# V of two batches loaded in four DMAs each, and casts on VectorE moved to earlier half-steps

## The chip, the cores and the metric

The kernel runs on one NeuronCore of a Trainium2 chip. The metric is the device time of the whole kernel in microseconds (us), median over several runs. The names of the engines are those of the profile: PE is the matrix engine, PEld its weight loads, DVE is VectorE, ACT is ScalarE, POOL is GpSimd, SP is SyncE, which here only issues DMAs.

## What is computed

Eight batches of attention with eight heads, 576 positions and head dimension 64, each query seeing itself and the 63 keys before it; the result, laid out as 4608 tokens of width 512, goes through two matrix products with an activation between them.

```python
scores = scale * q @ k.T ; scores = where((i - j >= 0) & (i - j < 64), scores, -1e9)
attn = softmax(scores) ; x = (attn @ v) as [4608, 512]
h = x @ w_in                       # [4608, 2048]
out = (h - tanh(h)) @ w_out        # [4608, 512]
```

Inputs and the output are float32. The kernel computes in bf16 with float32 sums.

## The kernel before

**Units of work.** A batch `b` has four pairs of heads; pair `pr` of batch `b` is unit `g = 4 b + pr`. The tokens are cut into nine chunks `c` of 512. For every chunk there are 16 steps `m` of the hidden layer: `hp_mm(c, m)` (four matrix products, L383), the tanh on ACT (L388), and `g_sub(c, m)`, the subtraction on DVE (L395) that writes `gT`. The second product (L407) reads `gT` and `w_out_sb`.

**The order.** The schedule is written out by hand. The program counts half-steps `h`. In `OPS`, step `m` of chunk 0 is at `h = 2 m`, step `m` of chunk 1 at `h = 32 + 2 m`. `at(h, fn, ...)` hangs other work on a half-step. In a half-step the matrix products and the tanh are recorded first, then what hangs there in the order of the `at` calls, and then the subtraction; each engine runs its instructions strictly in that order. Ahead of half-step 0 stands a prologue that does all of batch 0 (units 0 to 3).

**From DRAM to the matrix engine.** POOL issues the loads of q, k and v, which turn float32 into bf16 on the way: `load` one pair of q or k (L96), `load_v_all` the whole V of a batch (L135), `load_v` one pair of V (L143). All V of a batch goes to one tile, `vall`, of which there is one buffer. `cast_pair(g, eng)` copies k and q of unit `g` into rows that PE can transpose (`kb`, `qb`), `cast_v(b, pr, eng)` copies a pair of V into `vb`; both show at L85, on DVE or on POOL. When all four pairs of `vb` are there, `keys_v` sends it to `vw` in nine DMAs (L165), on POOL's and SP's queues in turn. `shift_dve(b, 0, 4)` copies `vw` by one block on DVE (L171), and `tile_pv` (L304) reads it. `tr_rows` transposes `kb` and `qb` on PE (L269), `tile_scores` is the score product and the exponential (L288, L291).

**Batch 1** (units 4 to 7): its V is loaded by the prologue, behind the first half of `w_in` (`wi`, one of two DMAs of L180) and ahead of units 4 and 5, the second half of `w_in`, and units 6 and 7. Its four `cast_v` hang on half-steps 1, 3, 5 and 9, `cast_pair` of unit 4 on 8, of unit 5 on 11, of units 6 and 7 on 16. `keys_v` of batch 1 is on 9, `shift_dve` on 18. The second half of `w_in` is first read by step `m = 8`, on half-step 16.

**Batch 2** (units 8 to 11): on half-step 9 POOL issues its V and then k and q of units 8 to 11. On half-step 21 POOL does its four `cast_v` and the casts of unit 8, which `tr_rows` of unit 8 needs on half-step 31. On half-step 23 come its `keys_v`, then `w_out` in two DMAs (L188) and q, k and V of batch 3 as three whole loads.

**The eight lanes of POOL's DMAs.** The built program gives each DMA of POOL's queue one of eight semaphores in turn (DMASW0 to DMASW7). A DMA therefore waits at POOL until the DMA eight places before it in POOL's queue has landed, and whatever stands behind it on POOL, DMAs and casts, waits too.

Of the kernel before, what the change touches and what calls it, by code (L numbers as in the profile page):

```python
# [15 lines left out]
def kernel(  # L16
# [11 lines left out]
    NP = H // 2  # L28
# [104 lines left out]
    def load_v_all(b):  # L133
        t = v_pool.tile([PV, H, EV * D], BF16, tag="v", name="vall")
        nc.gpsimd.dma_start(out=t, in_=v[b].rearrange("h (p e) d -> p h (e d)", e=EV))  # L135
        for pr in range(NP):
            stage[b, pr, "v"] = t[:, pr::NP]

    def load_v(b, pr):
        if (b, "v") not in whole:  # L140
            whole[b, "v"] = v_pool.tile([PV, H, EV * D], BF16, tag="v", name="vall")
        t = whole[b, "v"][:, pr::NP]
        nc.gpsimd.dma_start(out=t, in_=v[b, pr::NP].rearrange("h (p e) d -> p h (e d)", e=EV))  # L143
        stage[b, pr, "v"] = t
# [18 lines left out]
    def keys_v(b, j, eng=nc.sync):  # L163

        eng.dma_start(out=vw[b % 2][64:128, j].rearrange("p h c -> p (h c)"),  # L165
                      in_=vb[8 * j:8 * j + 8].rearrange("p e h c -> p e (h c)"))
# [12 lines left out]
    def load_w_in(i):  # L179
        nc.gpsimd.dma_start(out=w_in_sb[i], in_=w_in_r[:, :, 1024 * i:1024 * i + 1024])  # L180
# [260 lines left out]
    def at(h, fn, *args):  # L441
        items.setdefault(h, []).append((fn, args))
# [10 lines left out]
    V, A, G, Y = nc.vector, nc.scalar, nc.gpsimd, nc.sync  # L453
# [23 lines left out]
    for j, eng in enumerate((G, G, G, Y, G, Y, G, Y, G)):  # L477
        keys_v(0, j, eng)
    load_w_in(0)
    load_v_all(1)  # L480
    for g in 4, 5:
        load(g, "k", G)
        load(g, "q", G)
# [37 lines left out]

    at(0, lambda: nc.vector.memset(vw[1][0:64, 0], 0.0))
    at(0, lambda: nc.vector.memset(qT[1], 0.0))
    for pr, h in enumerate((1, 3, 5, 9)):
        at(h, cast_v, 1, pr, V)
    at(9, lambda: [keys_v(1, j, (G, Y)[j % 2]) for j in range(NJ)])
    at(8, cast_pair, 4, V)
    at(11, cast_pair, 5, V)
    at(9, load_v_all, 2)
    for g in 8, 9, 10, 11:  # L530
        at(9, load, g, "k", G)
        at(9, load, g, "q", G)
# [42 lines left out]
    for g in range(2 * NP + 2, B * NP):  # L575
        b, pr = divmod(g, NP)
# [96 lines left out]
```

## Time and profile before

| what | us |
|---|---|
| median of 7 runs | 335.42 (333.59 to 337.11) |
| the profiled execution | 335.42 |
| its span in the profile | 333.7 |
| PE busy in the span | 314.9 (94%) |
| DVE, ACT, POOL busy | 198.7, 184.1, 115.2 |

The span runs from the first to the last instruction; all places in time below are us from its start. The timeline gives for each instruction its start, its duration, the engine, the line, what it writes and reads, and in brackets the idle time of the engine before it with what ended it. A row that ends with "to landing" says how long a DMA took from the start of its issue to its arrival.

Where the loads of POOL's queue were issued and when they landed in this execution (us):

| DMA | issued | landed |
|---|---|---|
| `wi`, first half | 14.05 | 25.4 |
| V of batch 1 | 15.24 | 28.9 |
| k4, q4, k5, q5 | 16.44, 17.09, 17.72, 18.41 | 29.6, 30.4, 31.1, 31.9 |
| `wi`, second half | 19.23 | 36.8 |
| k6, q6, k7, q7 | 20.01, 25.74, 29.19, 29.93 | 37.6, 38.8, 40.2, 41.4 |
| five `vw` of batch 1 | 33.59 to 37.85 | 41.6 to 42.7 |
| V of batch 2 | 39.16 | 46.6 |
| k8 | 40.74 | 47.0 |
| q11 (the last of batch 2) | 46.88 | 53.1 |

### The profile page before, as it was taken

The numbers are of one execution on the slowest core, as the hardware profiler recorded it, in microseconds if no ns is written. First come the engines' busy times: TensorE is split into PE (matmuls) and PEld (weight loads), VectorE is DVE, ScalarE is ACT, GpSimd is POOL, SyncE is SP. The second block draws the span as 40 slices with busy tenths as digits, with TensorE's granted clock in tenths as the row PEclk, the third lists the DMA queues.
The fourth block names the chain that finished last, engine by engine and source line by source line (L and its number), as shares of the span: only waits on it lengthen the run. The fifth ranks groups of instructions, "written<-read, shape, count | busy, mean of one in ns | idle before, by whom it ended". The sixth has DMA issues, their size and how long they took to land.

```text
span 333.7 us, 6238 instructions
## 1 busy us (share of the span) xinstructions
PE 314.9 (94%) x2408; PEld 175.7 (53%) x2439; DVE 198.7 (60%) x335; ACT 184.1 (55%) x337; POOL 115.2 (35%) x167
## 2 busy tenths in 40 slices
PE   6867999899999999999999999999999999999996
PEld 2544565455555655655555555555554444444444
DVE  4576597993347675767676766677666433444400
ACT  3644779583466666666566666555553444434411
POOL 8842589604940843631724493500000000000000
PEclk9589999999999999999999999999999999999999
DMA  8999996995698289575975977966104000100022
GB/s 159 164 173 206 165 181 110 187 201 105 123 185 167 28 150 216 111 110 136 145 152 116 157 139 159 200 155 167 55 33 102 34 31 35 60 33 31 31 82 78
DMA packets 47222, 40.68 MB, mean 122 GB/s; under 512 B 18632, under 2 KB 40584, under 8 KB 47000
## 3 DMA queue, kind: packets, MB, share of 16 engines
q0 software_dynamic: 21440, 19.73, 39.1%
q1 hardware_dynamic: 25544, 20.25, 23.8%
q8 instruction: 19, 0.31, 0.4%
q10 hardware_dynamic: 208, 0.29, 0.3%
q14 instruction: 11, 0.09, 0.1%
HBM read 36.70 MB, written 10.62 MB: 142 GB/s over the span
## 4 chain that ended last, share of the span: by engine, by line
PE 73%; DVE 9%; DMA 8%; ACT 3%; POOL 3%; issue 2%; DVEq 0%; POOLq 0%
PE ps L407 34%; PE ps L383 28%; DMA vall<-in_v_dram 4%; PE ps L332 3%; PE ps L316 3%; DVE gT L395 2%; DMA vw<-vb 2%; DVE xs L343 2%; PE ps L249 2%; DMA qall<-in_q_dram 2%; DVE qt L85 2%; ACT qt L83 1%; PE ps L422 1%; DVE vw L171 1%; POOL vb L85 1%
## 5 line engine op out<-in xcount | busy, mean ns | idle before, releaser
L383 PE MATMUL ps<-xT,wi 128*128 128x512 bf16 x576 | 147.1, 379 | 2.7 <-DMA wi<-in_moe_w_in_dram 1.2
L395 DVE TENSOR_TENSOR gT<-ps,th 128x512 bf16<-128x512 f32 x144 | 98.5, 689 | 69.9 <-ACT th L388 68.6
L407 PE MATMUL ps<-w_out_sb,gT 128*128 128x512 bf16 x531 | 135.6, 379 | 1.5
L388 ACT ACTIVATE th<-ps 128x512 f32<-128x512 f32 x144 | 86.0, 599 | 82.3 <-PE ps L383 79.4
L383 PEld LDWEIGHTS <-wi 128*128 128x128 bf16 x576 | 60.4, 113 | 47.6 <-issue 3.2
L407 PEld LDWEIGHTS <-gT 128*128 128x128 bf16 x560 | 52.2, 98 | 52.7 <-issue 0.5
L318 ACT ACTIVATE pt<-ps 128x384 bf16<-128x384 f32 x66 | 32.3, 490 | 23.8 <-PE ps L316 23.8
L85 POOL COPY vb<-vall 72x1024 bf16<-72x1024 bf16 x24 | 24.8, 1054 | 35.0 <-DMA vall<-in_v_dram 35.0
L343 DVE TENSOR_TENSOR xs<-ps,rc 64x576 bf16<-64x576 f32 x44 | 33.2, 755 | 1.1
L412 ACT ACTIVATE ysb<-ps 128x512 f32<-128x512 f32 x35 | 21.0, 599 | 18.9 <-PE ps L407 18.8
L85 DVE COPY qt<-ps 64x576 bf16<-64x576 bf16 x18 | 13.7, 760 | 24.1 <-ACT qt L83 24.1
L85 POOL COPY qb<-qall 96x768 bf16<-96x768 bf16 x23 | 19.5, 846 | 19.5 <-DVE pt L322 10.5
L332 PEld LDWEIGHTS <-pt 128*128 128x128 bf16 x198 | 16.5, 98 | 15.3 <-DVE pt L322 0.8
L332 PE MATMUL ps<-vw,pt 128*128 128x130 bf16 x198 | 22.0, 220 | 0.4 <-DVE pt L322 0.4
L316 PE MATMUL ps<-qt,kt 128*128 128x128 bf16 x198 | 21.8, 219 | 0.0
L316 PEld LDWEIGHTS <-kt 128*128 128x128 bf16 x198 | 15.4, 98 | 8.8 <-issue 0.2
L85 POOL COPY kb<-kall 96x768 bf16<-96x768 bf16 x23 | 19.5, 850 | 1.2 <-DMA kall<-in_k_dram 1.2
L322 DVE TENSOR_TENSOR pt<-pt,ps 128x1152 bf16<-128x1152 bf16 x22 | 16.4, 745 | 0.8 <-ACT pt L318 0.8
L83 ACT ACTIVATE kt<-ps 128x576 bf16<-128x576 bf16 x22 | 14.4, 653 | 1.6 <-PE ps L249 1.5
L291 ACT ACTIVATE pt<-ps 128x640 bf16<-128x640 f32 (+1 forms) x20 | 12.5, 647 | 3.1 <-PE ps L288 3.1
L96 POOL DMA_DIRECT2D qall<-in_q_dram x15 | 9.9, 662 | 8.0 <-DMA wi<-in_moe_w_in_dram 5.1
L83 ACT ACTIVATE qt<-ps 64x576 bf16<-64x576 bf16 x18 | 11.5, 637 | 1.4 <-PE ps L249 1.4
(76 smaller groups left out, 202.7 us busy)
## 6 DMA issues: line engine op xcount, KB each, us to landing
out_dram<-ysb SPq DMA_DIRECT2D x35, 256.0 KB
vall<-in_v_dram POOLq DMA_DIRECT2D x7, 576.0 KB, 12.2
vw<-vb SPq DMA_DIRECT2D x39, 65.0 KB
qall<-in_q_dram POOLq DMA_DIRECT2D x4, 576.0 KB, 12.4
kall<-in_k_dram POOLq DMA_DIRECT2D x4, 576.0 KB, 12.5
kall<-in_k_dram POOLq DMA_DIRECT2D x15, 144.0 KB, 6.3
qall<-in_q_dram POOLq DMA_DIRECT2D x15, 144.0 KB, 5.8
wi<-in_moe_w_in_dram POOLq DMA_DIRECT2D x2, 1024.0 KB, 14.5
```

The source lines that it names most:

```text
L83: nc.scalar.activation(o, i, ACT.Copy)
L85: eng.tensor_copy(o, i)
L316: nc.tensor.matmul(sp[:, i, :], kT[g % NK][:, 64 * j:64 * j + 128], qT[g % NR][:, :, 64 * j:64 * j + 64], start=True, stop=True)
L318: nc.scalar.activation(PT[g % NPT][:, 3 * grp:3 * grp + 3, :], sp, ACT.Exp, scale=scale)
L322: nc.vector.tensor_tensor(p, p, mask.unsqueeze(1).to_broadcast([128, 2 * NJ, 64]), ALU.mult)
L332: nc.tensor.matmul(ps[:, 5 + grp, 130 * i:130 * i + 130], PT[g % NPT][:, j, :], vw[b % 2][:, j, 2 * pr:2 * pr + 2, :], start=True, stop=True)
L343: nc.vector.tensor_tensor(xo[r, :, :, pr, :], ov[r, :, :, h, 0:D], rc[r].to_broadcast([64, 3, 3, 64]), ALU.mult)
L383: nc.tensor.matmul(hp, w_in_tile(ki, m), chunk_tile(c)[:, :, ki % 2, 64 * (ki // 2):64 * (ki // 2) + 64], start=(ki == 0), stop=(ki == 3))
L388: nc.scalar.activation(th, hp, ACT.Tanh)
L395: nc.vector.tensor_tensor(gT[c][:, m, :], hp, th, ALU.subtract)
L407: nc.tensor.matmul(yp, gT[c][:, m, s * 128:(s + 1) * 128], w_out_sb[:, m, :], start=(m == 0), stop=(m == M - 1))
L412: nc.scalar.activation(ysb, ps[:, yp_bank(c, s), :], ACT.Copy)
```

## The change

V of batches 1 and 2 is loaded by four `load_v`, one for each pair, where one `load_v_all` stood. Two `cast_v` of batch 1 move to half-step 0, ahead of the first subtraction, the other two to half-steps 1 and 3. `cast_pair` of unit 4 moves from half-step 8 to 5, of unit 5 from 11 to 9.

```diff
     load_w_in(0)
-    load_v_all(1)
+    for pr in range(NP):
+        load_v(1, pr)
     for g in 4, 5:
         load(g, "k", G)
         load(g, "q", G)
...
-    for pr, h in enumerate((1, 3, 5, 9)):
+    for pr, h in enumerate((0, 0, 1, 3)):
         at(h, cast_v, 1, pr, V)
     at(9, lambda: [keys_v(1, j, (G, Y)[j % 2]) for j in range(NJ)])
-    at(8, cast_pair, 4, V)
-    at(11, cast_pair, 5, V)
-    at(9, load_v_all, 2)
+    at(5, cast_pair, 4, V)
+    at(9, cast_pair, 5, V)
+    for pr in range(NP):
+        at(9, load_v, 2, pr)
     for g in 8, 9, 10, 11:
         at(9, load, g, "k", G)
         at(9, load, g, "q", G)
```

The order on DVE from the end of the prologue, before and after (s0 is the first subtraction, V0 to V3 are the casts of V, kt the copies of transposed k out of PSUM):

```
before: s0 V0 s1 V1 s2 V2 s3 k4 q4 s4 V3 kt4 s5 k5 q5 s6 kt5 s7 k6 q6 k7 q7 s8
after:  V0 V1 s0 V2 s1 V3 s2 k4 q4 s3 s4 k5 q5 kt4 s5 s6 kt5 s7 k6 q6 k7 q7 s8
```

On POOL the one DMA of V becomes four in two places and nothing else moves; with it, the lane on which each later DMA waits moves by three. PE, ACT and SP keep their order.

## The prediction

> **What bounds the kernel now.** I read the busy shares, then PE's timeline over half-steps 0 to 31, then the landings of the DMAs that PE waits for, then POOL's timeline. First PE's row and its row of slices:
>
> ```profile
> PE 314.9 (94%) x2408; PEld 175.7 (53%) x2439; DVE 198.7 (60%) x335; ACT 184.1 (55%) x337; POOL 115.2 (35%) x167
> PE   6867999899999999999999999999999999999996
> ```
>
> PE is the bound; only its gaps can be won. Two rows of the windows (duration, then busy time by engine) show what the changed half-steps hold:
>
> ```profile
> 25.50:32.10 6.60, 5.53 (x24) 2.63 (x24) 4.01 (x10) 3.38 (x6) 1.91 (x3) 1.00 1.22 206
> 32.10:36.90 4.80, 4.27 (x55) 2.61 (x55) 4.31 (x10) 2.58 (x5) 2.17 (x3) 1.00 1.04 175
> ```
>
> PE idles 1.07 and 0.53 us there, DVE is busy 4.31 of 4.80. That speaks for the change. Now PE's timeline, the rows that count:
>
> ```profile
> 32.14 0.43 PE L269 MATMUL ps<-ident,kb 96*128 96x96 bf16 x6 [1.11 <-DVE kb L85]
> 36.55 0.43 PE L269 MATMUL ps<-ident,qb 96*128 96x96 bf16 x6
> 36.90 1.05 PE L383 MATMUL ps<-xT,wi 128*128 128x512 bf16 x4
> 42.50 1.02 PE L383 MATMUL ps<-xT,wi 128*128 128x512 bf16 x4 [0.24 <-DVE gT L395]
> 52.36 0.43 PE L269 MATMUL ps<-ident,kb 96*128 96x96 bf16 x6 [0.24 <-POOL kb L85]
> ```
>
> The gap at 32.14 is the wait for DVE's cast of k4. But 36.90 is step m = 8, the first that reads the second half of w_in, and that DMA has only just come:
>
> ```profile
> L180 POOL DMA_DIRECT2D wi<-in_moe_w_in_dram x1: 778/778/778, 19.2 to 19.2; - x1
> DMA to landing us min/median/max: 17.6/17.6/17.6
> ```
>
> 19.23 + 17.6 = 36.83, 0.07 before PE starts. So PE is on time for its data at 36.90; whatever it gains earlier, it waits for there. From 36.90 to 52.12 it idles 0.24 us once, at 42.50, for s8, which stands on DVE behind the cast of q7 (landed 41.4). At 52.36 it waits 0.24 for POOL's cast of k8. POOL up to there:
>
> ```profile
> 39.16 0.84 POOL L135 DMA_DIRECT2D vall<-in_v_dram  x1 [0.75 <-DMA qall<-in_q_dram]
> 40.74 0.67 POOL L96 DMA_DIRECT2D kall<-in_k_dram  x1 [0.74 <-PE ps L269]
> 41.95 0.65 POOL L96 DMA_DIRECT2D qall<-in_q_dram  x1 [0.54 <-PE ps L288]
> ...
> 45.18 0.63 POOL L96 DMA_DIRECT2D kall<-in_k_dram  x1
> 46.88 0.63 POOL L96 DMA_DIRECT2D qall<-in_q_dram  x1 [1.07 <-DMA vall<-in_v_dram]
> 47.51 4.03 POOL L85 COPY vb<-vall 72x1024 bf16<-72x1024 bf16 x4
> 51.48 0.82 POOL L85 COPY kb<-kall 96x768 bf16<-96x768 bf16 x1
> ```
>
> Ten issues, then four casts of V, then k8: an unbroken chain, and PE already waits at its end. The gaps at 40.74 and 41.95 are the lanes of k7 and q7 (landed 40.2 and 41.4), whatever releaser the row names; the one at 46.88 is V's own lane.
>
> **The change part by part.** *Casts on DVE.* V's casts last 0.42 us each on DVE, those of k and q 0.35 (0.34 and 0.27 from start to start). From the table of landings POOL's loads land in order of issue: V took the stream from 25.4 to 28.9, so I estimate pieces at 26.3, 27.2, 28.0 and 28.9. V0 and V1 are then done at 27.6, before s0, which started at 28.08 because its tanh was ready then. After it: V2, s1 (29.1), V3 (29.8 to 30.1), s2, k4 and q4 (30.75 to 31.3, landed at 29.6 and 30.4), s3, s4, k5 and q5 (32.6 to 33.1, landed 31.9). vb is complete at 30.1 in place of 33.3, k4 comes 1.0 us sooner, k5 about 1.9. PE's 1.6 us of gaps largely go, and PE stands at m = 8 near 35.4. There it waits for w_in until 36.83: gain 0.07 at most. The next tie is s8 behind q7's landing, gain 0; the next is k8 from POOL, the third part. So this edit I cost at nothing; what hides it is the second half of w_in. If that cover were gone, it would be worth up to 1.6 us. The other way: a piece of V that lands late holds s0 behind V1; up to some 1.4 us of that is covered by the same wait.
>
> *V of batch 1 in four.* A piece of V in the prologue cost POOL 0.68 to 0.83 us to issue (0.69 taken), the whole 0.85: 4 x 0.69 - 0.85 = 1.9 us more. Three more DMAs also shift the lanes: q5 now waits for the first half of w_in (lands 25.4) and is issued near 25.7, not 18.4; w_in's second half waits for V0 (26.3) and is issued near 26.6, not 19.2; k6, q6, k7, q7 near 27.5, 28.3, 29.2 and 29.95 (before: 20.0, 25.7, 29.2, 29.9). Cover: the stream was full until 41.4, and w_in's turn comes when q5 has landed, 31.9. Its issue ends at 27.4, 4.5 us ahead. So cost nothing; with the cover gone, each us of delay at w_in is one us at 36.90, of which the part that PE waits at 52.36 anyway is free. The vw DMAs on SP start some 3 us sooner, but must pass through the same stream before q7 either way; those on POOL stay behind q7 in the queue, and fourth and fifth wait for w_in and k6 as before (three more DMAs stand ahead of both, so the lanes fall alike).
>
> Here a rule speaks against the change. The Trainium skill, "SBUF — State Buffer", section "Who interferes with whom", says that a DVE copy in a two-port mode and GpSimd exclude each other for the whole instruction, and that descriptor generation counts as GpSimd's work. The trace has such a case:
>
> ```profile
> 58.95 1.22 POOL L135 DMA_DIRECT2D vall<-in_v_dram  x1
> 59.10 3.23 DVE L171 COPY vw<-vw 64x2080 bf16<-64x2080 bf16 x2
> ```
>
> The issue took 1.22 where others take 0.84, the two copies 3.23 where shift_dve of batch 0 took 1.52. By the rule the six casts that now fall between 26 and 31.5 can each hold an issue for one cast, 0.35 to 0.42: some 2 us on POOL in all, still within the 4.5 of cover. By the row, 0.4 for one collision. Both give 0 in the sum.
>
> *V of batch 2 in four.* This one has no cover. V0 goes at 39.16 as before (lane of q6), V1 on k7's lane at 40.5 to 40.7, V2 on q7's at 41.75 to 41.95, V3 at once, done 43.1 to 43.3. Then eight loads at 0.645: seven end at 47.6 to 47.8. The last, q11, waits for the lane of V3. Before, the two gaps at 40.74 and 41.95 were also there, but between them POOL issued k8 and q8; these now come after. When V3 lands isn't in the trace. Lower bound: the whole V landed at 46.6, then there is no wait. Upper: k10 flew 7.2 us, giving 49.7. Nearest rows: the pieces in the prologue flew 5.1 to 5.4, q8 to q9 5.6 to 5.8 in a full queue; I take 5.2 from 42.5, so 47.7, and 0.3 from landing to issue as at 46.56 to 46.88. Then q11 is issued at 48.0, the casts of V begin at 48.6, k8 at 52.6 and is ready near 53.4. Before: 47.51, 51.48, 52.3. POOL is 1.1 us later (0.75 without any wait for V3), and PE, in front of this wait before, is later by the same 1.1.
>
> Here too a rule is to hand: the Trainium skill, "DMA: Bandwidth & Descriptors", "Anatomy of one DMA — SWDGE (gpsimd) path", fits a DMA as about 2.0 us plus its bytes at 436 GB/s. Three more DMAs would be 6 us if one followed the other, against 3 x 0.65 of POOL's time by the rows. The landings in a full queue (k8 47.0, q8 47.6, k9 48.3) are 0.6 to 0.7 apart, so the fixed part overlaps; I count issue time only.
>
> Behind 52.36 everything hangs on the same POOL chain or on PE: qb8, five vw, w_out (landed 66.7 and 71.9, first read 75.20), the loads of batch 3. All shifts together, so nothing is given back. **Sum:** 0 + 0 + 1.1 = +1.1 us on the profiled execution of 335.42, which equals the median: 336.5.
>
> **The rivals.** *A, forecast:* the gain stops at w_in, POOL pays near k8: 336.5, own range 335.4 to 337.6; chance 0.55.
>
> *B, slower by more than the bound:* V3 of batch 2 lands late and the lane holds q11, and behind it the four casts and k8. With the 5.2 us as 7.2, as k10 flew, q11 goes at 50.0, POOL is 3.1 late: 338.5. It decides once V3 flies longer than about 5.8 us (casts begin after 49.2). For it: flights of 5.6 to 7.2 in that stretch. Against: V's pieces would have fewer loads ahead of them than k10 had. Chance 0.23.
>
> *C, a changed meeting of shift_dve and POOL at 59:* the copies start 1.1 us before POOL's casts at 60.17. A few tenths of drift frees them (gain about 1.5 of PE's waits at 62 to 65: 335.0) or catches both copies (loss about 1.9: 338.4). In the trace both sides hang on k8, so drift is small. Chance 0.12, split evenly.
>
> *D, faster:* the profile's own chain runs through V's landing at 28.9, vb and vw to 42.1. If that is the true path, and w_in and POOL do not hold it back, all of PE's gaps from 25.5 to 52.4 could go, 1.07 + 0.53 + 0.24 + 0.24 = 2.1: 333.3. Against: 36.83 beside 36.90, and the chain on POOL. Chance 0.10.
>
> **How the numbers follow.** A measurement of this kernel tells about 0.5%, 1.7 us, from no change: below 333.7 is faster, above 337.1 slower. Faster: D, and a little of C, 0.11. Slower: B 0.23, C's loss 0.06, and A's upper end 0.07: 0.36. Same: 0.53. The range takes A whole, B to just above its price, and most of C: 334.2 to 338.6, which leaves out D and a longer flight.
>
> **What would show it.** Right: PE at m = 8 still starts near 36.9, now after a wait of over 1 us for w_in; kb8 at PE near 53.4 with a wait of over 1 us on POOL; POOL's casts of batch 2 near 48.6; the loads still landing in order. Wrong: m = 8 near 35.5 (w_in was no gate), k8 cast before 51.5, or w_in landing after 38 (the late issue did starve the stream).

## Result and the profile after

The changed kernel took 336.28 us (median of 27 runs) against 335.78 for the kernel before (64 runs beside it): ratio 1.0019, 95% interval 1.0003 to 1.0035. That is 0.6 us more, within what I called no change; the forecast was 1.1 us more. A second set of 22 runs gave 0.9997 (0.9972 to 1.0022). The first profile of the changed kernel fell in a disturbed execution, so what is read below is the profile of that second set (called the rerun, span 334.5 us).

The page of the rerun, its busy shares and PE's slices:

```profile
PE 318.6 (95%) x2439; PEld 176.9 (53%) x2439; DVE 199.7 (60%) x335; ACT 184.3 (55%) x337; POOL 118.7 (35%) x173
PE   7877998799999999999999999999999999999996
```

POOL is busy 3.5 us more than before (118.7 against 115.2): six more DMA issues of 0.6 to 0.7, and little besides. PE's sum can't be compared with the 314.9 of before, because 31 matmul records are missing there (x2408 against x2439).

PE's timeline in the rerun, at the same places as before:

```profile
25.92 5.37 PE L383 MATMUL ps<-xT,wi 128*128 128x512 bf16 x24 [1.97 <-DMA wi<-in_moe_w_in_dram]
...
32.84 1.02 PE L383 MATMUL ps<-xT,wi 128*128 128x512 bf16 x4 [0.77 <-DVE gT L395]
...
36.93 1.05 PE L383 MATMUL ps<-xT,wi 128*128 128x512 bf16 x4 [0.46 <-DMA wi<-in_moe_w_in_dram]
...
52.99 0.43 PE L269 MATMUL ps<-ident,kb 96*128 96x96 bf16 x6 [1.08 <-POOL kb L85]
```

The wait of 1.11 us for DVE's cast of k4 is gone. In its place stands a wait of 0.77 for a subtraction (0.17 before), and then, at step m = 8, a new wait of 0.46 that names the DMA of w_in. That DMA:

```profile
L180 POOL DMA_DIRECT2D wi<-in_moe_w_in_dram x1: 764/764/764, 26.8 to 26.8; - x1
DMA to landing us min/median/max: 10.1/10.1/10.1
```

It was issued at 26.8, 7.6 us later than before, and landed at 36.9, as before: its later issue cost nothing. Between the waits at 36.93 and 52.99 PE ran without a pause. The wait for POOL's cast of k8 grew from 0.24 to 1.08. POOL's timeline ahead of it:

```profile
40.08 3.03 POOL L143 DMA_DIRECT2D vall<-in_v_dram  x4 [0.96 <-DMA qall<-in_q_dram]
43.10 0.67 POOL L96 DMA_DIRECT2D kall<-in_k_dram  x1
...
47.51 0.64 POOL L96 DMA_DIRECT2D qall<-in_q_dram  x1
48.14 4.04 POOL L85 COPY vb<-vall 72x1024 bf16<-72x1024 bf16 x4
52.11 0.82 POOL L85 COPY kb<-kall 96x768 bf16<-96x768 bf16 x1
```

Twelve issues without a gap (before: nine, with three gaps), then the casts: POOL's own issue time reaches from the landing of q6 to the casts. They begin at 48.14 (before: 47.51, forecast 48.6). But the first of these rows stands at 40.08, where it stood at 39.16 before, because q6 landed later. The account of the prediction below comes back to this.

### The profile page after: what moved, and what is told of

It is laid out like the page before. It is cut to its first block, busy times and chain, and to the rows that moved or that the text cites. A ratio compares the mean times of both kernels' runs of the same rounds, so it can differ in the third digit from the quotient of the medians.

```text
span 337.2 us, 6244 instructions
## 1 busy us (share of the span) xinstructions
PE 316.5 (94%) x2408; PEld 176.8 (52%) x2439; DVE 199.4 (59%) x335; ACT 184.2 (55%) x337; POOL 119.3 (35%) x173
## 4 chain that ended last, share of the span: by engine, by line
PE 72%; DMA 10%; DVE 8%; POOL 4%; ACT 3%; issue 2%; DVEq 0%; POOLq 0%
PE ps L407 31%; PE ps L383 30%; DMA vw<-vb 6%; DMA wi<-in_moe_w_in_dram 4%; PE ps L332 3%; DVE gT L395 2%; PE ps L316 2%; DVE xs L343 2%; PE ps L249 2%; DVE qt L85 1%; PE ps L422 1%; POOL vw L165 1%; DVE vw L171 1%; POOL vall L143 1%; PE ps L269 1%
## 5 line engine op out<-in xcount | busy, mean ns | idle before, releaser
L383 PE MATMUL ps<-xT,wi 128*128 128x512 bf16 x576 | 148.6, 383 | 5.5 <-DMA wi<-in_moe_w_in_dram 3.7
L332 PEld LDWEIGHTS <-pt 128*128 128x128 bf16 x198 | 16.5, 98 | 15.5 <-DVE pt L322 0.8
L332 PE MATMUL ps<-vw,pt 128*128 128x130 bf16 x198 | 22.2, 220 | 0.5 <-DVE pt L322 0.4
L165 POOL DMA_DIRECT2D vw<-vb x17 | 10.1, 601 | 6.0 <-DMA wi<-in_moe_w_in_dram 2.8
```

The costliest lines, as they stand in the source:

```text
L332: nc.tensor.matmul(ps[:, 5 + grp, 130 * i:130 * i + 130], PT[g % NPT][:, j, :], vw[b % 2][:, j, 2 * pr:2 * pr + 2, :], start=True, stop=True)
L383: nc.tensor.matmul(hp, w_in_tile(ki, m), chunk_tile(c)[:, :, ki % 2, 64 * (ki // 2):64 * (ki // 2) + 64], start=(ki == 0), stop=(ki == 3))
```

## The experiments

| run | what differs from the kernel before | ratio | 95% interval |
|---|---|---|---|
| again | the whole change | 0.9997 | 0.9972 to 1.0022 |
| v2_only | V of batch 2 in four | 1.0034 | 1.0013 to 1.0054 |
| v2_eight | V of batch 2 in eight | 1.0073 | 1.0048 to 1.0099 |
| front_only | batch 1's part | 1.0010 | 0.9986 to 1.0035 |
| casts_only | the moved casts alone | 1.0040 | 1.0005 to 1.0076 |
| front_wi2 | batch 1's part, w_in's second half in two | 1.0008 | 0.9981 to 1.0035 |
| swap_casts | the change, k8 and q8 cast ahead of V | 1.0112 | 1.0067 to 1.0157 |
| after_late11 | the change, k11 and q11 loaded later | 1.0033 | 1.0011 to 1.0055 |
| before_pace | a wait on POOL ahead of the casts of unit 10 | 1.0044 | 1.0013 to 1.0076 |
| before_dve | casts of units 10 and 11 on DVE | 0.9996 | 0.9965 to 1.0027 |
| after_dve | the change, casts of 10 and 11 on DVE | 1.0030 | 1.0006 to 1.0055 |
| dve_v3_first | before_dve, V of batch 3 first | 0.9944 | 0.9920 to 0.9968 |

One caution for all the profiles: the first half of w_in landed anywhere from 23.6 to 26.3 us in these runs, also among kernels that do not differ up to that point. One span therefore says little about a half per cent; I use the ratios for time, and the profiles for which wait stands where, and for stretches inside one profile.

**The whole change, again** (no edit).

> The changed kernel itself, once more, for a profile beside the other parts. Theory T (PE's gain ends at the wait for the second half of w_in; POOL's three extra issues for batch 2 delay the cast of k8): +0.6 to +1.1 us against before; the first half of w_in lands near 25.4 as before, PE starts step m = 8 near 36.9 after a wait of over 1 us, and waits 1.0 to 1.4 us for POOL's cast of k8. Rival R (the four pieces of V run beside the first half of w_in and hold it back): w_in's first half lands near 27.9 again, as in the first profile of the changed kernel, all later places are some 2 us later, and PE has no wait at m = 8.

T's waits are there (0.46 at m = 8, not over 1; 1.08 at k8); the time, within -0.9 to +0.7 us of the kernel before, tells little of T's 0.6 to 1.1. w_in's first half landed at 25.9, so the 27.9 of the first profile was not the rule.

**V of batch 2 alone (v2_only).**

```diff
-    at(9, load_v_all, 2)
+    for pr in range(NP):
+        at(9, load_v, 2, pr)
```

> Only V of batch 2 in four DMAs; batch 1 as before. T: all of the loss is here: +0.7 to +1.2 us; POOL's casts of batch 2 begin 0.7 to 1.2 us later than before measured from the landing of q7, and PE's wait for k8 grows from 0.24 to about 1.2. R: the loss is in batch 1, so 0 here, within 0.3 us.

+0.34%, 1.1 us: as T said. POOL's timeline of this run, then PE's wait:

```profile
37.78 0.70 POOL L143 DMA_DIRECT2D vall<-in_v_dram  x1 [0.87 <-DMA qall<-in_q_dram]
39.26 0.69 POOL L143 DMA_DIRECT2D vall<-in_v_dram  x1 [0.77 <-DMA kall<-in_k_dram]
40.28 1.63 POOL L143 DMA_DIRECT2D vall<-in_v_dram  x2 [0.33 <-DMA qall<-in_q_dram]
...
46.97 0.63 POOL L96 DMA_DIRECT2D qall<-in_q_dram  x1 [0.65 <-DMA vall<-in_v_dram]
47.62 4.03 POOL L85 COPY vb<-vall 72x1024 bf16<-72x1024 bf16 x4
```

```profile
52.47 0.43 PE L269 MATMUL ps<-ident,kb 96*128 96x96 bf16 x6 [1.77 <-POOL kb L85]
```

The pieces stand in the gaps that the lanes of k7 and q7 leave, where k8 and q8 stood before; the loads behind them are pushed on, and the last waits 0.65 us on the lane of the fourth piece. From q6's landing (37.5) to the casts it is 10.1 us; before, 38.8 to 47.51, 8.7. So POOL is 1.4 us later (1.5 from q7's landing, where T had 0.7 to 1.2), and PE's wait 1.5 us longer. All of the mechanism that I forecast is in these rows.

**V of batch 2 in eight (v2_eight)**, one DMA for each head, issued in the order of the pairs:

```diff
-    at(9, load_v_all, 2)
+    at(9, load_v_heads, 2)   # for pr: for h in (pr, pr + NP): dma_start(out=t[:, h], in_=v[b, h]...)
```

> As before, but V of batch 2 in eight DMAs, one for each head. It doubles the suspected cost. T (POOL's issue time for the extra DMAs stands in front of the cast of k8): seven extra issues of 0.65 us; less the gaps that POOL had, the casts of batch 2 begin about 3.4 us later than before and PE waits for k8 by as much: +3 to +3.8 us (about +1.0%), against +1.1 us for four. If the cost were that of splitting as such (a fixed time of the last piece's landing), it would stay near +1.1 to +1.5.

+0.73%, 2.5 us: more than double v2_only's, as a cost for each issue would have it. The middle is below the 3 to 3.8 expected; the interval, 1.6 to 3.3 us, reaches into it.

```profile
40.13 0.56 POOL L533 DMA_DIRECT2D vall<-in_v_dram  x1 [1.01 <-DMA qall<-in_q_dram]
41.22 0.56 POOL L533 DMA_DIRECT2D vall<-in_v_dram  x1 [0.53 <-DMA kall<-in_k_dram]
42.25 3.30 POOL L533 DMA_DIRECT2D vall<-in_v_dram  x6 [0.46 <-DMA qall<-in_q_dram]
50.58 4.03 POOL L85 COPY vb<-vall 72x1024 bf16<-72x1024 bf16 x4
```

```profile
55.44 0.43 PE L269 MATMUL ps<-ident,kb 96*128 96x96 bf16 x6 [2.75 <-POOL kb L85]
```

A one-head piece took 0.55 us to issue where I had taken 0.65, and no lane held the last load. PE's wait for k8 is 2.75: 0.24 whole, 1.77 in four, 2.75 in eight. No DMA's landing held POOL behind the first pieces, so with batch 1 as before the price of splitting is POOL's issue time ahead of k8.

**Batch 1's part alone (front_only)**: the change without its last edit.

> Only batch 1's part: its V in four, its casts earlier; V of batch 2 in one DMA. T: 0 to -0.3 us: PE stands at m = 8 over 1 us before w_in's second half has landed and waits for it; k8 as before. R: +0.6 us or more, with w_in's first half late by about 2 us. If V's landing was the true path: -1 to -2 us, and PE's m = 8 near 35.5.

1.0010, an interval of 0.9986 to 1.0035: no gain of 1 to 2 us, so V's landing was not the true path. T's sign of it, a wait at m = 8, does not show in this profile, because PE was slowed: its first 24 products took 7.06 us, against 5.37 in the rerun (granted clock 0.85 in the stretch from 25.5 to 36.9, 1.00 in the rerun). PE came to m = 8 at 37.99, 1 us behind w_in. The sign does show in all four other runs that have the new front at full clock: 0.46 (again), 0.70 (swap_casts), 1.04 (after_late11) and 1.07 (after_dve). Two runs with the old front show it too, 0.50 (v2_eight) and 0.29 (before_dve): there w_in held PE even without the change.

**The moved casts alone (casts_only)**: V of batch 1 in one DMA, the four `at` lines of the casts as in the change.

> Only the moved casts; V of batch 1 in one DMA, V of batch 2 as before. V lands about 3.4 us after w_in's first half, so the two casts ahead of the first subtraction now hold it back by about 1.7 us. T: the wait for w_in's second half covers it, PE starts m = 8 at its landing as before: 0 to +0.5 us. If nothing covers it (the DVE chain is the true path): +1.5 us or more.

+0.40%, 1.3 us, between T's 0 to 0.5 and the 1.5 or more of a missing cover; the interval, 0.2 to 2.6 us, takes in both. PE's first tie in this run:

```profile
28.80 2.07 PE L383 MATMUL ps<-xT,wi 128*128 128x512 bf16 x8 [1.09 <-DVE gT L395]
```

The first subtraction stands behind two casts that wait for the whole V (27.4 us), and PE waits 1.09 us for it. From there to m = 8 it did not wait for w_in (35.6 us, PE at 35.97), and its wait for k8 was 0.81. The cover that I had counted on was there only in part. The four DMAs spare PE this wait of 1.09; that the kernel's time gains by them isn't shown, since the intervals of casts_only and front_only overlap.

**w_in's second half in two (front_wi2)**: front_only, with `load_w_in(1)` as two DMAs of 512 columns.

> Batch 1's part of the change, with w_in's second half in two DMAs of 512 columns, so that steps 8 to 11 need only the first of them, which lands some 2.4 us sooner. V of batch 2 as before. T: PE no longer waits at m = 8, and starts it about 10 us after the landing of w_in's first half in place of 11; but the next ties (the subtraction behind the cast of q7, the vw DMAs of batch 1, and POOL's cast of k8) stand where they were, so the time moves by no more than 0 to -0.4 us, and PE's wait for k8 grows by what was gained at m = 8. If w_in alone had held PE: -1 us or more.

1.0008 (0.9981 to 1.0035), as T said: there is no gain of 1 us or more, so w_in alone does not hold the time. The place of m = 8 tells nothing, since PE was slow here too (7.06 us for the first 24 products), and stood at 37.67 when the first part of w_in had landed at 34.1.

**k8 and q8 ahead of V on POOL (swap_casts).**

```diff
-    at(21, lambda: [cast_v(2, pr) for pr in range(NP)])
     at(21, cast_pair, 8, G)
+    at(21, lambda: [cast_v(2, pr) for pr in range(NP)])
```

> The changed kernel with POOL's casts of k8 and q8 ahead of its four casts of V of batch 2. The sum of POOL's casts ahead of the vw DMAs is the same. T: k8 is ready four casts (4 us) sooner, PE no longer waits for it, and the loss of the change goes: -0.8 to -1.3 us against the changed kernel, 0 to -0.4 against before, unless POOL's vw DMAs (same place in its chain) make shift_dve of batch 2 the next wait, then part of it comes back there (up to 1 us). R: nothing changes at k8's side that the time shows; +0.6 against before as for the changed kernel.

+1.1%: a clear miss. PE no longer waits for k8, but DVE's two copies of shift_dve wait for vw, and PE behind them. POOL's, DVE's and PE's rows:

```profile
49.35 0.82 POOL L85 COPY kb<-kall 96x768 bf16<-96x768 bf16 x1 [1.97 <-DVE gT L395]
```

```profile
59.59 0.70 DVE L171 COPY vw<-vw 64x2080 bf16<-64x2080 bf16 x1 [1.79 <-DMA vw<-vb]
65.91 0.70 DVE L171 COPY vw<-vw 64x2080 bf16<-64x2080 bf16 x1 [5.62 <-DMA vw<-vb]
```

```profile
66.66 0.49 PE L304 MATMUL ps<-vw,pt 128*64 128x65 bf16 x10 [6.00 <-DVE vw L171]
```

POOL's vw DMAs landed at 61.3 at the latest. SP's four wait for the last cast of V, which now ends after k8 and q8; they were issued until 58.3, just when POOL issued w_out (58.18). The views print no landing for SP's DMAs, but the packed trace has their semaphore updates: three of the four are complete by 61.1, the last, issued from 57.4 on, at 65.8, just ahead of the second copy. That the 2 MB of w_out held it is inferred. V's casts themselves begin at 50.89, 2.75 us later than in the rerun. 1.97 of that is a new wait of POOL, for k8's own landing (49.2, whatever the row names), which V's casts had covered. So V ahead of k8 does two things: it covers k8's flight, and it gives SP's DMAs their lead.

**Two issues fewer ahead of k8 (after_late11).**

```diff
-    for g in 8, 9, 10, 11:
+    for g in 8, 9, 10:
...
+    at(23, load, 11, "k", G)
+    at(23, load, 11, "q", G)
     at(23, load_w_out, 0)
```

> The changed kernel with the loads of k11 and q11 issued by POOL behind the vw DMAs of batch 2 and not ahead of its casts. It takes two issues of 0.64 us out of the chain in front of the cast of k8, and the last load no longer waits there for the last piece of V. T (POOL's issues in front of k8 are the loss): POOL's casts of batch 2 begin 1.2 to 1.3 us sooner, PE's wait for k8 (1.08 in the rerun of the changed kernel) goes to 0 or 0.1: about -1 us against the changed kernel, and 0 to -0.8 against before. If the loss lies elsewhere: 0 to +0.8 against before, as the changed kernel.

POOL did as forecast: its casts begin at 46.98 (rerun 48.14), and PE does not wait for k8 at all. The time did not follow: 1.0033. PE's timeline has the waits that came in its place:

```profile
37.11 1.05 PE L383 MATMUL ps<-xT,wi 128*128 128x512 bf16 x4 [1.04 <-DMA wi<-in_moe_w_in_dram]
...
64.00 1.02 PE L383 MATMUL ps<-xT,wi 128*128 128x512 bf16 x4 [1.18 <-DVE gT L395]
...
100.85 0.27 PE L332 MATMUL ps<-vw,pt 128*128 128x130 bf16 x2 [0.56 <-DMA vw<-vb]
```

At 64.00 DVE is late, because a masking of 0.48 us took 1.68 beside POOL's casts. At 100.85 PE waits for V of batch 3. swap_casts and after_late11 together changed my picture: the wait for k8 is a real price when it is the last one, but there are two more ties behind it. The last four runs went after these.

**POOL's casts after DVE's copies (before_pace).**

```diff
+    at(44, pace, 42)
     at(44, cast_pair, 10, G)
```

> The kernel before, with one small copy on POOL ahead of the casts of unit 10 that waits for the subtraction behind shift_dve of batch 2 (pace(42) at half-step 44). So POOL casts after DVE's two copies and not beside them. In all profiles so far PE waits 0.9 to 1.6 us for these copies, whose second lasts 2.6 us in place of 0.7. Theory: that is the meeting of the two engines, the copies take 1.4 us, and PE's waits behind them (0.86, 0.37, 0.33 before) go: -1.0 to -1.6 us. Rival: the copies wait for their data, and it stays as it is: 0.

+0.44%, where a gain was expected. DVE's timeline and PE's:

```profile
59.30 1.57 DVE L171 COPY vw<-vw 64x2080 bf16<-64x2080 bf16 x2
...
62.51 2.86 DVE L295 TENSOR_TENSOR pt<-pt,mask_sb 128x512 bf16<-128x512 bf16 x1
```

```profile
66.41 0.51 PE L304 MATMUL ps<-vw,pt 128*64 128x65 bf16 x20 [2.68 <-DVE xs L310]
```

The copies went from 3.23 to 1.57 us, as said, and the next DVE operation with both inputs in SBUF, the masking at 62.51, took 2.86 in place of 0.45: POOL's four casts, 61.97 to 65.1, now met that one. So the meeting of the engines is real, and it moves to whatever stands there.

**These casts on DVE (before_dve and after_dve).**

```diff
-    at(44, cast_pair, 10, G)
-    at(50, cast_pair, 11, G)
+    at(33, cast_pair, 10, V)
+    at(35, cast_pair, 11, V)
```

> The kernel before, with the casts of units 10 and 11 on DVE (half-steps 33 and 35, 0.35 us each, in a stretch where DVE has 2 us of idle time) and not on POOL. With POOL's four casts gone from 60 to 64, no DVE operation meets them: shift_dve of batch 2 takes 1.4 to 1.6 us in place of 3.2, and, other than in the run with the pace, no masking meets them either. Theory (the meeting of the engines costs PE 0.9 + 0.4 + 0.3): -1.0 to -1.6 us. Rival (DVE itself holds PE there, and 1.2 us more of it costs what is won): 0, within 0.4.

> The changed kernel with the same move of the casts of units 10 and 11 to DVE. Theory: as in the run on the kernel before, -1.0 to -1.6 us against the changed kernel, so -0.4 to -1.4 against before; PE's wait for k8 stays at about 1.1. If k11 and q11 (landed 53 to 54) come after DVE wants them, DVE waits and part of it is lost, up to 0.5.

Both missed: 0.9996 and 1.0030. In before_dve the copies took 1.53 us and the masking 0.41, and PE came to the first vw product of batch 3 (L332) at 96.04; before, 97.68. Then:

```profile
101.02 0.27 PE L332 MATMUL ps<-vw,pt 128*128 128x130 bf16 x2 [2.27 <-DMA vw<-vb]
```

The gain of 1.6 us is gone within 5 us, and after_dve has the same at 102.80 (2.11 us). V of batch 3 landed at 81.0, POOL cast it until 85.8, and SP's DMAs of vw went out until 92.0. By its semaphore updates the last of them was complete at 101.0; in the kernel before at 99.7, about half a us ahead of the product that reads it. So there was little more than that to gain here. This chain starts with w_out's issue on POOL and hangs on the DMA stream, not on PE.

**The same with V of batch 3 first (dve_v3_first).**

```diff
     at(23, load_all, 3, "q")
+    at(23, load_v_all, 3)
     at(23, load_all, 3, "k")
-    at(23, load_v_all, 3)
...
-    VALUES = {3: (66, 1, 71), ...
+    VALUES = {3: (66, 0, 71), ...
```

> The kernel before with the casts of units 10 and 11 on DVE, as in the run before_dve, and V of batch 3 loaded ahead of its k, with its four casts on POOL ahead of the cast of k of unit 12. In before_dve PE stood 1.6 us ahead at the first vw product of batch 3 (96.0 us) and lost 2.3 us at its third, on a vw DMA that landed at 101.0. Theory (the landing of V of batch 3, 81 us, and POOL's casts behind it set that): V lands near 78, its casts end near 82 and not 86, vw lands near 98, PE does not wait there, and the gain of before_dve stays: -1.0 to -1.6 us against before. Rival: k of batch 3, now last (81), or another tie right behind takes it back: 0.

0.9944 (0.9920 to 0.9968), 1.9 us faster than the kernel before, and the only version here that beats both kernels. Its rows, POOL's, DVE's and PE's:

```profile
78.88 4.04 POOL L85 COPY vb<-vall 72x1024 bf16<-72x1024 bf16 x4 [2.58 <-DMA vall<-in_v_dram]
```

```profile
59.10 1.54 DVE L171 COPY vw<-vw 64x2080 bf16<-64x2080 bf16 x2
```

```profile
98.46 0.33 PE L332 MATMUL ps<-vw,pt 128*128 128x130 bf16 x3
```

V's four casts end at 82.9, and PE goes through its third group of products of unit 12 (98.46) without a wait. That the move to DVE alone isn't enough is shown by before_dve; V of batch 3 first without the move wasn't run.

## Why the prediction was right, point by point

**w_in holds m = 8: right, its size too large.** The DMA's landing stands in front of PE's start in four runs. The term that was mis-sized is "PE's 1.6 us of gaps largely go, and PE stands at m = 8 near 35.4": in the rerun it was ready at 36.47, of which 0.4 is w_in's first half that came later. The gap at k4 (1.11) went, but 0.77 came back at the next product, which waits for the fifth subtraction (s4 in the order on DVE). I had followed DVE's new order and not asked what PE's product behind k4 waits for. It cost nothing, as the wait for w_in covers it. front_wi2, which was to take this wait away, can't confirm the gate, since PE was slow there.

**V of batch 1 in four at nothing: right within the interval** (front_only, 0.9986 to 1.0035), with one assumption not borne out. I had the pieces land one after the other behind w_in. In the rerun the first came 0.6 us after w_in's first half, and the last at 28.2, no later than a whole V. In the six profiles with four pieces w_in's first half landed at 24.6 to 26.3 (mean 25.6), in the seven with a whole V at 23.6 to 25.5 (mean 24.5). That the pieces take some of its stream would fit, but the ranges overlap; it stays open. The second half, issued up to 8 us later, did not starve: 36.2 to 38.0 against 35.3 to 37.6. Of the 2 us that the casts on DVE could have cost POOL's issues by the rule cited, the rerun shows at most 0.5: gaps of 0.15, 0.22 and 0.16 between 27.5 and 30.8, and issues of 0.63 to 0.76, about as long as elsewhere.

**V of batch 2 in four: right where it stands alone, by luck in the whole change.** Forecast: POOL 1.1 us later, 0.75 to 3; v2_only gave 1.4 on POOL and 1.1 in time, by the steps forecast. The fourth piece flew 5.7 us there and 5.0 in the rerun (5.2 taken). The "ten issues" ahead of the casts before are nine in the rows; no sum rests on that. In the whole change POOL came 0.6 us later by other steps. The prediction had V0 "at 39.16 as before (lane of q6)", but q6 landed at 39.8 and not 38.8, 2.9 us behind w_in's second half in place of 2.0. q7, at 41.1, came no later than before (41.4), so POOL's gaps closed, and no lane held the last load. From q6's landing to the casts it is 8.3 us; with V whole it was 8.7 before and 8.6 in front_only, where V's own lane holds q11:

```profile
40.15 0.84 POOL L135 DMA_DIRECT2D vall<-in_v_dram  x1 [1.06 <-DMA qall<-in_q_dram]
...
47.84 0.63 POOL L96 DMA_DIRECT2D qall<-in_q_dram  x1 [1.63 <-DMA vall<-in_v_dram]
48.49 4.04 POOL L85 COPY vb<-vall 72x1024 bf16<-72x1024 bf16 x4
```

So in the profiles the four pieces cost POOL nothing beside batch 1's part; what came late came from q6.

It comes with the moved casts. casts_only, which changes no load, has q6 2.7 us behind w_in too. In the six profiles with the old casts k6 lands 0.4 to 0.9 us and q6 1.6 to 2.3 behind w_in's second half, in the seven with the new ones 1.2 to 1.5 and 2.7 to 2.9. SP's vw DMAs of batch 1 wait for the casts of V. Their first is issued 4.8 to 7.1 us ahead of w_in's landing with the new casts, and 3.5 to 4.1 with the old. That they take the stream ahead of k6 and q6 would fit; it isn't tested alone. The prediction saw these DMAs and asked only whether they pass before q7. Thus a term put at nothing, the moved casts, made POOL start 0.9 us later, the term put at 1.1 was nothing beside it (the stretch is 0.3 shorter), and the sum came out close. In time this can't be told apart: front_only's interval, -0.5 to 1.2 us, takes in both 0 and 0.9.

**"All shifts together, so nothing is given back": not tested by the change.** w_out and all behind it stand on the same POOL chain and shift with it, so the tie at 101, V of batch 3, never showed. It shows as soon as PE alone is moved: after_late11, before_dve and after_dve each took away 1 us or more at 52 to 66 and got nothing. Read the other way round, as what mending k8 would bring, the forecast of 1.1 us would have been wrong.

**The rivals.** B (the lane holds the last load for 2 us more) did not happen: 0.65 in v2_only, none in the rerun. C: wherever POOL cast straight behind its loads of batch 3, the copies met these casts, 2.4 to 4.0 us in place of 1.5 (swap_casts is the exception, where they came 6 us apart). The rerun has 3.36 against 3.23 before, so the change altered nothing there. D (V's landing as the true path, 2.1 us faster) falls with front_only.

## What to carry to other kernels

Before you credit a gap that you close, find the next instruction of the same engine that waits for something from another queue, here a weight DMA that had landed 0.07 us ahead of its reader, with no idle time to show for it. Splitting a DMA can pay only if someone uses the first piece early: for batch 1 it let casts start early, and nothing measurable came of it; for batch 2 the casts stood behind all the issues anyway. What an extra issue costs depends on the gaps beside it: v2_only paid 1.4 us on POOL for the three, and in the whole change they filled gaps and cost nothing. So the costs of two edits that share a queue can't simply be added. Where removing a wait brings nothing, look for the same microseconds at the next wait; here the casts' move to DVE alone brought nothing measurable, and with V of batch 3 first the two gave 0.56%.

## What was unexpected of the hardware

A DVE operation that meets a row of POOL copies can be held for longer than one of them: 2.86 us for a masking of 0.45 while POOL ran four copies of 0.81 to 0.82 each. The Trainium skill, "SBUF — State Buffer", section "Who interferes with whom", has whoever issues first hold the shared pair of ports "for the whole instruction" while the other is blocked; here DVE stayed blocked over more than one POOL instruction. In the kernel before, too, POOL's first two copies beside DVE kept their 0.84 and 0.83 us, and only the third and fourth were longer (1.31 and 1.17).

The first 24 products of the hidden layer took 5.4 us with a granted clock of 1.00 and 7.06 in front_only and front_wi2, where 0.76 was granted over them (5.37 / 0.76 = 7.07). That is 1.7 us from one run to the next, more than the effect studied here.
